# Half weight loads, a short sum on GpSimd and a conditional block without ScalarE, in a kernel of attention and routed experts

## The chip, the core and the metric

The kernel runs on one core of a Trainium2 chip. Its engines work side by side, each on its own queue of instructions: TensorE (PE; its weight loads are shown apart as PEld), VectorE (DVE), ScalarE (ACT), GpSimd (POOL) and SyncE (SP). SP and POOL also issue DMA transfers, which run on the core's 16 DMA engines. The metric is the time of one execution on the device, in microseconds; lower is better. Before the change it is 411.5 us, the median of three runs (409.78, 411.5, 412.72).

## The reference

First comes attention over 8 batches of 8 heads, 576 positions and 64 columns a head, causal by blocks of 64 positions:

```python
scores = scale * np.matmul(q, k.transpose(0, 1, 3, 2))
scores = np.where(block_i >= block_j, scores, -1000000000.0)
attn = np.exp(scores - max);  attn = attn / (sum + 1e-09)
attn_out = np.matmul(attn, v)
```

Its output, as 8 x 576 rows of 512 columns, goes through one expert a row. Each of the 8 experts has a w1 of 512 x 1024 and a w2 of 1024 x 512. Which expert takes a row is found in order within a batch: a local gate decides whether the row takes its own best expert or that of the row before it.

```python
logits = x @ w_gate;  local_gate = sigmoid(x @ w_local)
e = argmax(logits[s]) if s == 0 or local_gate[s] < 0.5 else prev_e
out[s] = softmax(logits[s])[e] * (np.maximum(x[s] @ w1[e], 0.0) @ w2[e])
```

## The kernel before

**Attention: slots.** Two heads of one batch make a pair; there are 32 pairs, four a batch. The loop at L1198 has one slot for each pair. Slot i computes the scores of pair i (L972 to L977), takes their exponentials on ScalarE (L987), forms the products with v of pair i - 1 (`values`, L998 and L1007), and transposes q and k of pair i + 1 (L692, L925, L946). SyncE loads q and k of pair i + 2 (L867, L872) and v (L889, L892). GpSimd arranges q and k of pair i + 2 (`arrange`, L880). The exponentials of the first block of keys are in a tile S, those of the other blocks in a tile Pc. S rotates through three buffers and Pc through two.

**Sums of rows.** The denominators of the softmax are found by a matrix product over S (`half_batch`, L705), in every odd slot, for the pairs i - 3 and i - 2. So that S holds the whole sum, VectorE adds the other blocks onto it in `add_chunks`: three sums of the wide blocks (L1019), and one short sum of 64 x 128 elements for the last block (L1021), whose exponentials lie in the lower half of S's first 64 columns. `mask` then clears that corner of S with a memset (L1026). Slot i masks pair i - 1. GpSimd does it for 30 of the pairs: in even slots up to 16 ahead of `arrange`, in the others behind it. VectorE does it for pair 29 (in slot 30) and for pair 31 (after the loop).

**Routing.** The choice of experts is a long chain of small steps (`tokens`, `slots_first`, `slots_second`), written as a generator. The loop gives its steps to VectorE and TensorE by a fixed budget of weights at fixed points of each slot (L1145, `vector`, `routing`). Finished rows are transposed by TensorE (`rows_of_batch`), scaled by VectorE (L818) and stored to a buffer `x_rows` in HBM (L677). These stores are held back and issued by GpSimd at the end of a slot (`release`, L1262). The scores, the transposes for rows and the small products of the routing share three PSUM buffers, "sc".

**Weights.** w1 and w2 of all experts are kept in SBUF as bf16. `load_weights` (L105) loads one w1 (L107) or w2 (L111) of one expert by one DMA of GpSimd's queue, which casts from f32: 1024 KB as written. Experts 0 to 6 are loaded in the loop, one load in every second slot from 2 to 28, in the order w1 of expert 0, w2 of expert 0, w1 of expert 1 and so on (L1258). What the routing needs as scratch lies in the place of expert 7, and staged q and k lie in those of experts 6 and 7 of w2. So expert 7 comes last: its w1 out of the list `pending`, between the first gathers, as soon as the routing has the row indices of the first phase (L540, issued at L1255 of slot 29), its w2 at the end of slot 30 (L1270). The order on GpSimd's queue at the end of a slot is:

```python
            while pending:
                pending.pop(0)()

            if wload < 2 * E - 2 and i == 2 + 2 * wload:
                load_weights(*divmod(wload, 2))
```

and behind it `release`.

**Experts: tiles.** Rows are gathered by expert into tiles of 128 rows, by indirect DMAs of GpSimd (L651), and transposed by DMAs of SyncE (L1269, L1393). A tile takes 32 products with w1 (`first_mm`, L1093), a ReLU on ScalarE (L1096), eight products with w2 (`second_mm`, L1335), a scaling on ScalarE (L1340) and an indirect store by GpSimd (L1343). VectorE copies the w1 of the tile's expert, chosen by a register, to a fixed place ahead of it (L1078, L1297). As the expert is in a register, the first products with w2 wait for all loads of w2. TensorE does the first products of tiles 0 and 1 about the end of the loop and those with w2 behind them.

**The conditional block.** The number of tiles depends on the data. The last five possible tiles are in a conditional block (`more_tiles`, L1417), run if the count of tiles in use is high enough. It stands in the loop over tiles four tiles ahead of the last one of the list. All engines load the count (L1473) and branch on it (L1474). `xtrans` (L1081), which copies transposed rows out of PSUM, is called in this block alone; `first_mm` and `second_mm` are called in the block and in the loop.

Of the kernel before, what the change touches and what calls it, by code (L numbers as in the profile page):

```python
# [62 lines left out]
def kernel(  # L63
# [11 lines left out]
    nc = tc.nc  # L75
# [4 lines left out]
    ALU = mybir.AluOpType  # L80
# [21 lines left out]
    w1_bf = w_p.tile([P, E * KO1 * F], BF16, tag="w1", name="w1_bf")  # L102
    w2_bf = w_p.tile([P, E * FO * Dm], BF16, tag="w2", name="w2_bf")
    WE = KO1 * F
    def load_weights(e, layer):  # L105
        if layer == 0:
            nc.gpsimd.dma_start(  # L107
                out=w1_bf[:, e * WE:(e + 1) * WE].rearrange("p (do f) -> p do f", f=F),
                in_=moe_w1[e].rearrange("(do di) f -> di do f", di=P))
        else:  # L110
            nc.gpsimd.dma_start(  # L111
                out=w2_bf[:, e * WE:(e + 1) * WE].rearrange("p (fo d) -> p fo d", d=Dm),
                in_=moe_w2[e].rearrange("(fo fi) d -> fi fo d", fi=P))

    HP = H // 2
    NPAIR = B * HP
# [715 lines left out]
    with tc.tile_pool(name="atn_const", bufs=1) as cst, \  # L832
# [181 lines left out]
        def add_chunks(i):  # L1014
            if not 0 <= i < NPAIR:
                return
            for c in range(1, NC - 1):
                n = S - P * c
                nc.vector.tensor_add(Ss[i][:, :, P * c:], Ss[i][:, :, P * c:],  # L1019
                                     Pc[i % 2][:, :, POS[c]:POS[c] + n])  # L1020
            nc.vector.tensor_add(Ss[i][ST:, :, LAST:], Ss[i][ST:, :, LAST:], Ss[i][ST:, :, :ST])  # L1021

        def mask(i, engine):

            if 0 <= i < NPAIR:
                engine.memset(Ss[i][ST:, :, :ST], 0.0)  # L1026

        def sums_of(i):
# [52 lines left out]
        def xtrans(x, ps, xT):  # L1081
            for ko in range(KO1):
                nc.tensor.transpose(ps[:, ko, :], x[:, ko * P:(ko + 1) * P], id_b)
            nc.scalar.copy(xT, ps)
            return xT

        def first_mm(xT, w, hT, bank2, between=lambda: None):
            for half in range(2):
                ps = bank2()
                for fo in range(FO // 2):  # L1090
                    f0 = (half * (FO // 2) + fo) * P
                    for ko in range(KO1):
                        nc.tensor.matmul(ps[:, fo, :], lhsT=w[:, ko * F + f0:ko * F + f0 + P],  # L1093
                                         rhs=xT[:, ko, :],
                                         start=(ko == 0), stop=(ko == KO1 - 1))
                relu[0] = nc.scalar.activation(  # L1096
                    hT[:, half * (FO // 2):(half + 1) * (FO // 2), :], ps, func=AF.Relu)
                between()
            return hT

# [97 lines left out]
        for i in range(NPAIR):  # L1198
# [56 lines left out]
            while pending:  # L1255
                pending.pop(0)()

            if wload < 2 * E - 2 and i == 2 + 2 * wload:  # L1258
                load_weights(*divmod(wload, 2))
                wload += 1  # L1260
            if i < NPAIR - 1:
                release(queue=nc.gpsimd)  # L1262
# [28 lines left out]
    with ExitStack() as ffn:  # L1291
# [40 lines left out]
        def second_mm(ph, j, hT, ev, factor, y=None, between=lambda: None):  # L1332
            ps = f_ps.tile([P, Dm], F32, tag="ps_y", name="ps_y")
            for fo in range(FO):
                nc.tensor.matmul(ps, lhsT=hT[:, fo, :],  # L1335
                                 rhs=w2_bf[:, bass.ds(ev + fo * Dm, Dm)],
                                 start=(fo == 0), stop=(fo == FO - 1))
# [76 lines left out]
        def part(o, n, k):  # L1414
            return old[:, o:o + n].rearrange("p (k n) -> p k n", k=k)

        def more_tiles():  # L1417

            o = WE + Dm + FO * P
            x, y = (old[:, o:o + 2 * n].bitcast(F32) for n in (XW, Dm))  # L1420
            factor = old[:, o + 2 * Dm:o + 2 * Dm + 2].bitcast(F32)
            for ph, j in more:
                e = expert(ph, j)

                nc.vector.memset(x, 0.0)
                gather(ph, j, x)
                w = weights_at(old[:, :WE], e)
                nc.vector.tensor_copy(factor, factor_of(x))
                xT = xtrans(row_of_x(x), ps_x(), part(WE, Dm, KO1))
                hT = first_mm(xT, w, part(WE + Dm, FO * P, FO), ps_h)  # L1430
                second_mm(ph, j, hT, e, factor, y)


        holding[0] = True
        for i, (ph, j) in enumerate(tiles):
# [34 lines left out]
            if i == behind_tile:  # L1470

                nc.gpsimd.drain()
                n = nc.values_load(used[0:1, 0:1], min_val=0, max_val=E * BS)  # L1473
                with tc.If(n > NS[1] - MORE, label="more"):  # L1474
                    more_tiles()
        i = len(tiles) - 1
# [37 lines left out]
```

## Time and profile before

| | us |
|---|---|
| median of three runs | 411.5 |
| profiled execution | 408.54 |
| its span in the profile | 406.5 |
| busy: TensorE | 392.6 (97%) |
| busy: VectorE | 242.2 (60%) |
| busy: ScalarE | 228.7 (56%) |
| busy: GpSimd | 196.1 (48%) |

Times within the profile are counted from the start of the span. The attention loop takes about the first 257 us, the experts the rest. The granted clock of TensorE is at full speed in all slices. In a row of a timeline stand the start, the length, the engine, the line, the operation, the tile written and those read; at its end, in brackets, stand how long the engine had been idle before it and what ended that. "q" behind an engine's name is its sequencer, which issues instructions, waits and branches. q0 is the DMA queue of GpSimd, q1 that of SyncE; its row gives packets, MB and the share that the packets took of the 16 engines' time.

### The profile page before, as it was taken

Reading aid. Unit: us, or ns where it says so; the run is one execution under the profiler, and the core shown is the slowest. Engines: PE = TensorE matmul, PEld = TensorE weight load, DVE = VectorE, ACT = ScalarE, POOL = GpSimd, SP = SyncE. Lnnn points to the kernel's source line nnn. Section 1 sums busy time; section 2 is a strip of 40 time slices with the busy share of each in tenths; the row PEclk is TensorE's granted clock in tenths of the full one; section 3 lists DMA queues with packets and bytes.
Section 4 is the critical chain, followed back from the end, with each engine's and each line's share of the span. In section 5 each row is a group of like instructions: output and inputs, shape, how many; then the busy total and the mean of one; then the engine's idle time right before and its main releaser. Section 6 shows DMA issues by size and latency. Waiting matters only on the chain. (4 is left out here: it accounts for less than half of the span.)

```text
span 406.5 us, 14547 instructions
## 1 busy us (share of the span) xinstructions
PE 392.6 (97%) x5834; PEld 285.5 (70%) x5834; DVE 242.2 (60%) x505; ACT 228.7 (56%) x391; POOL 196.1 (48%) x250
## 2 busy tenths in 40 slices
PE   9999999999999999999998998998999999999985
PEld 7667677677677677667766666666777777777763
DVE  2463564564564577967899975977887333333320
ACT  3758557567557557657647465333545555555542
POOL 1244251342341342582632363074776888888833
PEclk9999999999999999999999999999999999999999
DMA  6588989999999979999989689944763645655532
GB/s 178 142 190 194 216 172 222 201 201 228 194 202 210 183 183 246 174 202 244 170 192 237 136 155 192 151 109 120 166 168 97 170 135 148 154 149 149 128 99 78
DMA packets 108819, 69.97 MB, mean 172 GB/s; under 512 B 74847, under 2 KB 100255, under 8 KB 108752
## 3 DMA queue, kind: packets, MB, share of 16 engines
q0 software_dynamic: 19200, 34.84, 41.6%
q1 hardware_dynamic: 89552, 34.19, 37.2%
q8 instruction: 48, 0.79, 0.8%
q14 instruction: 19, 0.16, 0.1%
HBM read 66.88 MB, written 14.70 MB: 201 GB/s over the span
## 5 line engine op out<-in xcount | busy, mean ns | idle before, releaser
L1019 DVE TENSOR_TENSOR S<-S,Pc 128x896 f32<-128x896 f32 (+2 forms) x96 | 84.0, 875 | 23.9 <-PE o L998 19.1
L977 PE MATMUL sc<-qkT 64*64 64x224 f32 (+6 forms) x1536 | 91.6, 367 | 0.0
L1297 DVE COPY w1c<-w_bf 128x4096 bf16 x36 | 44.3, 1231 | 55.6 <-PE ps_h L1093 52.8
L1093 PEld LDWEIGHTS <-w1c 128*128 128x128 bf16 x1152 | 67.2, 98 | 9.1 <-issue 1.3
L880 POOL COPY w_bf<-w_bf 128x512 f32<-128x512 f32 x61 | 43.9, 737 | 60.8 <-DMA w_bf<-in_k_dram 33.0
L977 PEld LDWEIGHTS sc<-qkT 64*64 64x64 f32 x1536 | 70.5, 134 | 3.7 <-issue 2.5
L1335 PE MATMUL ps_y<-w_bf,hT 128*128 x296 | 69.9, 379 | 1.0 <-DMA w_bf<-in_moe_w_dram 1.0
L987 ACT ACTIVATE Pc<-sc 128x448 f32<-128x448 f32 (+1 forms) x96 | 68.1, 716 | 0.0
L1093 PE MATMUL ps_h<-xT,w1c 128*128 128x128 bf16 x1088 | 66.3, 219 | 1.3 <-ACTq L1474 1.1
L1343 POOL DMA_INDIRECT out_dram<-y,idx x37 | 56.2, 1519 | 22.0 <-ACT y L1340 12.2
L651 POOL DMA_INDIRECT xg<-x_rows,idx x38 | 47.1, 1239 | 31.3 <-issue 13.9
L1096 ACT ACTIVATE hT<-ps_h 128x512 bf16<-128x512 f32 x76 | 45.3, 597 | 26.2 <-PE ps_h L1093 24.6
L998 PE MATMUL o<-Pc,v 128*64 128x320 f32 (+2 forms) x512 | 57.3, 366 | 0.0
L998 PEld LDWEIGHTS o<-Pc,v 128*64 128x64 f32 x512 | 34.6, 137 | 24.1
L1340 ACT ACTIVATE y<-ps_y,xg 128x512 f32<-128x512 f32 x37 | 25.4, 687 | 45.5 <-PE ps_y L1335 39.1
L987 ACT ACTIVATE S<-sc 128x576 f32<-128x576 f32 x64 | 42.0, 656 | 12.6 <-PE sc L977 12.1
L1335 PEld LDWEIGHTS <-hT 128*128 128x128 bf16 x296 | 27.5, 98 | 27.3 <-issue 1.0
L1011 ACT COPY oT<-o 128x576 f32<-128x576 f32 x32 | 20.5, 641 | 35.7 <-PE o L1007 35.7
L1026 POOL MEMSET S<- 64x128 f32 x30 | 6.0, 200 | 69.8 <-DVE S L1021 40.7
L818 DVE TENSOR_TENSOR xg<-trx,rs 128x512 bf16<-128x512 f32 (+1 forms) x31 | 20.2, 685 | 25.9 <-PE trx L692 25.8
L998 PE MATMUL o<-S,v 128*64 128x192 f32 (+1 forms) x256 | 34.7, 392 | 0.3 <-ACT qkT L925 0.3
L714 ACT COPY LT<-trg 128x320 f32<-128x320 f32 x15 | 6.4, 426 | 44.4 <-PE trg L705 44.4
(313 smaller groups left out, 467.4 us busy)
## 6 DMA issues: line engine op xcount, KB each, us to landing
w_bf<-in_moe_w_dram POOLq DMA_DIRECT2D x16, 1024.0 KB, 9.9
w_bf<-in_k_dram SPq DMA_DIRECT2D x32, 256.0 KB, 3.4
w_bf<-in_q_dram SPq DMA_DIRECT2D x32, 256.0 KB, 7.7
v<-in_v_dram SPq DMA_DIRECT2D x64, 128.0 KB, 5.8
x_rows<-xg POOLq DMA_DIRECT2D x24, 128.0 KB, 8.1
qkl<-in_k_dram SPq DMA_DIRECT2D x32, 32.0 KB, 3.8
qkl<-in_q_dram SPq DMA_DIRECT2D x32, 32.0 KB, 5.7
vl<-in_v_dram SPq DMA_DIRECT2D x32, 32.0 KB, 7.4
```

The source lines that it names most:

```text
L651: st = nc.gpsimd.indirect_dma_start(out=x, out_offset=None, in_=x_dram[:rows], in_offset=bass.IndirectOffsetOnAxis(ap=row_of(ph, j), axis= ...
L880: copies[j](m, raws[i][1 + j].rearrange("p h j d -> p j h d"))
L977: nc.tensor.matmul(to[:, col + skip:col + n], lhsT=t[r, 0, k0:k0 + ST], rhs=t[r, 1, q0 + skip:q0 + n], start=True, stop=True)
L987: nc.scalar.activation(exps_at(i, c, q0, n, rows), ps[rows, :, col:col + n], func=AF.Exp, scale=scale_attn)
L998: nc.tensor.matmul(po[64 * h:64 * h + 64, VO + q0:VO + q0 + n], lhsT=vs[i][c][:, h, :], rhs=exps_at(i, c, q0, n, slice(0, P))[:, h, :], st ...
L1019: nc.vector.tensor_add(Ss[i][:, :, P * c:], Ss[i][:, :, P * c:], Pc[i % 2][:, :, POS[c]:POS[c] + n])
L1093: nc.tensor.matmul(ps[:, fo, :], lhsT=w[:, ko * F + f0:ko * F + f0 + P], rhs=xT[:, ko, :], start=(ko == 0), stop=(ko == KO1 - 1))
L1096: relu[0] = nc.scalar.activation(hT[:, half * (FO // 2):(half + 1) * (FO // 2), :], ps, func=AF.Relu)
L1297: ended["w"] = nc.vector.tensor_copy(w, w1_bf[:, bass.ds(ev[i], WE)])
L1335: nc.tensor.matmul(ps, lhsT=hT[:, fo, :], rhs=w2_bf[:, bass.ds(ev + fo * Dm, Dm)], start=(fo == 0), stop=(fo == FO - 1))
L1340: nc.scalar.activation(y, ps, func=AF.Copy, scale=factor)
L1343: st = nc.gpsimd.indirect_dma_start(out=out_flat, out_offset=bass.IndirectOffsetOnAxis(ap=row_of(ph, j), axis=0), in_=y, in_offset=None, b ...
```

## The change

Three things are changed.

1. `load_weights` can load a half of a w1 or w2: the halves divide the rows of the matrix by the groups of 128 of them, so the runs in memory stay as long as they were. The 14 loads of the loop become 28 halves, one in each slot from 2 to 29. Expert 7 is loaded whole, as before.
2. The short sum (L1021) moves from `add_chunks` to `mask`, ahead of its memset and on the same engine: GpSimd for 30 pairs, VectorE for pairs 29 and 31.
3. In the conditional block the work of ScalarE (the copy in `xtrans`, the ReLU, the scaling) goes to VectorE, and ScalarE neither loads the count nor branches.

```diff
-    def load_weights(e, layer):
-        if layer == 0:
-            nc.gpsimd.dma_start(
-                out=w1_bf[:, e * WE:(e + 1) * WE].rearrange("p (do f) -> p do f", f=F),
-                in_=moe_w1[e].rearrange("(do di) f -> di do f", di=P))
-        else:
...
+    def load_weights(e, layer, half=None):
+        w, x, n = ((w1_bf, moe_w1, F), (w2_bf, moe_w2, Dm))[layer]
+        r = slice(0, WE // n) if half is None else slice(half * WE // n // 2, (half + 1) * WE // n // 2)
+        nc.gpsimd.dma_start(
+            out=w[:, e * WE:(e + 1) * WE].rearrange("p (o n) -> p o n", n=n)[:, r],
+            in_=x[e].rearrange("(o i) n -> i o n", i=P)[:, r])
...
-            nc.vector.tensor_add(Ss[i][ST:, :, LAST:], Ss[i][ST:, :, LAST:], Ss[i][ST:, :, :ST])
 
         def mask(i, engine):
 
             if 0 <= i < NPAIR:
+                engine.tensor_tensor(Ss[i][ST:, :, LAST:], Ss[i][ST:, :, LAST:],
+                                     Ss[i][ST:, :, :ST], op=ALU.add)
                 engine.memset(Ss[i][ST:, :, :ST], 0.0)
...
         def xtrans(x, ps, xT):
...
-            nc.scalar.copy(xT, ps)
+            nc.vector.tensor_copy(xT, ps)
...
-        def first_mm(xT, w, hT, bank2, between=lambda: None):
+        def first_mm(xT, w, hT, bank2, between=lambda: None, scalar=True):
...
+                if scalar:
+                    relu[0] = nc.scalar.activation(to, ps, func=AF.Relu)
+                else:
+                    nc.vector.tensor_single_scalar(to, ps, 0.0, op=ALU.max)
...
-            if wload < 2 * E - 2 and i == 2 + 2 * wload:
-                load_weights(*divmod(wload, 2))
+            if wload < 4 * E - 4 and i == 2 + wload:
+                load_weights(*divmod(wload // 2, 2), wload % 2)
                 wload += 1
...
-            nc.scalar.activation(y, ps, func=AF.Copy, scale=factor)
+            if scalar:
+                nc.scalar.activation(y, ps, func=AF.Copy, scale=factor)
+            else:
+                nc.vector.tensor_scalar(y, ps, factor, None, op0=ALU.mult)
...
+        MORE_ON = tuple(getattr(mybir.EngineType, e) for e in ("PE", "DVE", "Pool", "SP"))
...
-                hT = first_mm(xT, w, part(WE + Dm, FO * P, FO), ps_h)
-                second_mm(ph, j, hT, e, factor, y)
+                hT = first_mm(xT, w, part(WE + Dm, FO * P, FO), ps_h, scalar=False)
+                second_mm(ph, j, hT, e, factor, y, scalar=False)
...
-                n = nc.values_load(used[0:1, 0:1], min_val=0, max_val=E * BS)
+                n = nc.values_load(used[0:1, 0:1], min_val=0, max_val=E * BS, engines=MORE_ON)
                 with tc.If(n > NS[1] - MORE, label="more"):
                     more_tiles()
```

More of the change, by code (lines that the diff above doesn't have):

```diff
@@ L104 @@
     WE = KO1 * F
-    def load_weights(e, layer):
-        if layer == 0:
-            nc.gpsimd.dma_start(
-                out=w1_bf[:, e * WE:(e + 1) * WE].rearrange("p (do f) -> p do f", f=F),
-                in_=moe_w1[e].rearrange("(do di) f -> di do f", di=P))
-        else:
-            nc.gpsimd.dma_start(
-                out=w2_bf[:, e * WE:(e + 1) * WE].rearrange("p (fo d) -> p fo d", d=Dm),
-                in_=moe_w2[e].rearrange("(fo fi) d -> fi fo d", fi=P))
+    def load_weights(e, layer, half=None):
[4 more added lines that the diff above has]
+            in_=x[e].rearrange("(o i) n -> i o n", i=P)[:, r])
     HP = H // 2
@@ L1095, in first_mm @@
                                          start=(ko == 0), stop=(ko == KO1 - 1))
-                relu[0] = nc.scalar.activation(
-                    hT[:, half * (FO // 2):(half + 1) * (FO // 2), :], ps, func=AF.Relu)
+                to = hT[:, half * (FO // 2):(half + 1) * (FO // 2), :]
+                if scalar:
+                    relu[0] = nc.scalar.activation(to, ps, func=AF.Relu)
+                else:
+                    nc.vector.tensor_single_scalar(to, ps, 0.0, op=ALU.max)
                 between()
@@ L1330, in last_mm, with second_mm @@
             tc.add_to_no_dep_group("stores", st.ins)
-        def second_mm(ph, j, hT, ev, factor, y=None, between=lambda: None):
+        def second_mm(ph, j, hT, ev, factor, y=None, between=lambda: None, scalar=True):
             ps = f_ps.tile([P, Dm], F32, tag="ps_y", name="ps_y")
```

## The prediction

> **What bounds the kernel now.** I read the page first, then the list of what TensorE waited for, then the timelines of TensorE, VectorE and GpSimd around each of those waits, and last the DMA queues there.
>
> ```profile
> span 406.5 us, 14547 instructions
> PE 392.6 (97%) x5834; PEld 285.5 (70%) x5834; DVE 242.2 (60%) x505; ACT 228.7 (56%) x391; POOL 196.1 (48%) x250
> ```
>
> TensorE is busy for 392.6 of 406.5 us. So an edit on VectorE, ScalarE or GpSimd is worth only what it takes from, or adds to, the short list of TensorE's own waits (line, whom it waited for, us, times, longest):
>
> ```profile
> PE sc L975 <- DVE xg L818: 1.8, 1, 1.8
> PE ps_h L1093 <- ACTq L1474: 1.1, 1, 1.1
> PE rtb L340 <- DVE S L337: 1.0, 1, 1.0
> PE ps_y L1335 <- DMA w_bf<-in_moe_w_dram: 1.0, 1, 1.0
> ...
> PE rti L496 <- DVE w_bf L525: 0.2, 1, 0.2
> ```
>
> Each part of the change points at one of these. In time they stand here, with what ran ahead of them:
>
> ```profile
> 211.89 1.26 PE L705 MATMUL trg<-S,sel 128*32 128x320 f32 x16
> ...
> 216.63 0.67 PE L692 MATMUL trx<-id_f,oT 64*128 64x64 f32 x16
> ...
> 224.13 0.22 PE L975 MATMUL sc<-ones_b,minus 64*64 64x64 bf16 x2 [1.77 <-DVE xg L818]
> ...
> 262.69 1.89 PE L1335 MATMUL ps_y<-w_bf,hT 128*128 x8 [0.97 <-DMA w_bf<-in_moe_w_dram]
> ```
>
> From the first product to slot 28 no wait over 0.3 us is TensorE's, and none at all is for the q, k or v loads. What the change does there is covered; the sum is made at slots 26 to 31 and at the branch.
>
> **Part 1: the short sum leaves VectorE.** Of the 32 short sums (L1021), 30 go to GpSimd; those of pairs 29 and 31, which VectorE masks, stay on it. They are worth something where VectorE is late, which is the queue that ends in L818 ahead of 224.13. The first row groups the four sums between 189 and 218.3 us (min/median/max ns); the others are VectorE's timeline:
>
> ```profile
> L1021 DVE TENSOR_TENSOR S<-S x4: 289/400/511, 193.9 to 217.9; 64x128 f32<-64x128 f32 x4
> ```
> ```profile
> 189.56 0.68 DVE L818 TENSOR_TENSOR xg<-trx,rs 64x512 bf16<-64x512 f32 x1 [1.69 <-PE trx L692]
> ...
> 218.27 1.29 DVE L818 TENSOR_TENSOR xg<-trx,rs 128x512 bf16<-128x512 f32 x2
> ```
>
> VectorE waits last at 189.56 and then runs without a gap past 224. The four sums are 4 x 0.40 = 1.6 us of that queue. Not all of it comes through: the L818 at 218.27 needs the transposes that TensorE ends at 216.63 + 0.67 = 217.30, so it can come forward by 0.97 at most, and I take 0.9. All behind it shifts alike, so TensorE's 1.77 falls to about 0.9. One more short sum, that of slot 28, lies between there and L525, so the 0.2 of L496 goes too. **Gain 1.1 us** from 229 on; bounds 0 (GpSimd takes it back, below) and 2.0 (the whole 1.77 and 0.2).
>
> On GpSimd the sum has no row. The nearest are the memset behind it and a copy with four times its elements (the copy as min/median/max ns):
>
> ```profile
> 210.65 0.20 POOL L1026 MEMSET S<- 64x128 f32 x1 [0.29 <-DVE S L1021]
> ```
> ```profile
> L880 POOL COPY w_bf<-w_bf x61: 608/622/1292, 6.9 to 235.5; 128x512 f32<-128x512 f32 x61
> ```
>
> So 0.2 to 1.3 us, and I take 0.3, near the memset of its shape: 30 x 0.3 = 9 us more on an engine that is 48% busy. The new wait is GpSimd's, for the last L1019 sum; the memset waited for L1021, behind that, so it begins no later. Queued behind it are the memset, then the arranging copies or the weight load, and TensorE's row sums, which read the masked tile. The tightest place that I find is this memset against the L705 row at 211.89: it ends at 210.85, 1.0 us before the row sums. A sum of 0.3 is covered; without that cover TensorE pays what it takes over 1.0. The Trainium skill (GPSIMD Engine Reference, Engine selection) says that a two-input elementwise operation is about twice as slow on GpSimd and belongs on VectorE. By it the sum would take an estimated 0.6 us, twice the 0.29 of VectorE, still inside the cover; no row here shows a two-input operation on GpSimd.
>
> **Part 2: weight loads in halves.** 14 loads in slots 2, 4, ..., 28 become 28 in slots 2 to 29, so half a load sits in every slot and the second half of each pair comes one slot later. Their issues are 14 more. A whole one takes GpSimd 0.8 to 0.93, a 128 KB store 1.16 / 2 = 0.58:
>
> ```profile
> 241.76 0.83 POOL L107 DMA_DIRECT2D w_bf<-in_moe_w_dram  x1
> 242.90 1.04 POOL L651 DMA_INDIRECT xg<-x_rows,idx  x1 [0.30 <-issue]
> 244.25 1.01 POOL L651 DMA_INDIRECT xg<-x_rows,idx  x1 [0.31 <-issue]
> 246.66 1.16 POOL L677 DMA_DIRECT2D x_rows<-x  x2 [1.40 <-DVE x L818]
> ...
> 248.38 0.93 POOL L111 DMA_DIRECT2D w_bf<-in_moe_w_dram  x1
> ```
>
> Extra issue time is 14 x 0.6 to 0.9, about 8 to 13 us, in slots where GpSimd waits for others. It matters where the last half falls. That is the second half of w2 of expert 6, now in slot 29. In the code slot 29 first issues the pending gathers and the load of expert 7's w1 (the first three rows) and then this half, so it comes at about 245.3, into the idle 1.40 ahead of 246.66: the issue is covered. Its data is not. It stands in GpSimd's DMA queue ahead of the x stores and of expert 7's w2 (248.38), for which TensorE waits at 262.69. The queue in two stretches: 40 to 54 us, where it carries one whole w2 load and nothing else, and 244 to 262; then all engines from 250 to 262 and from 262 to 266 (last two columns: DMA share, GB/s):
>
> ```profile
> q0 software_dynamic: 1040, 1.05, 50.2%
> ```
> ```profile
> q0 software_dynamic: 1776, 2.66, 93.8%
> ```
> ```profile
> 250.00:262.00 12.00, 11.27 (x181) 8.77 (x181) 10.31 (x20) 6.19 (x13) 0.20 (x1) 1.00 1.29 182
> 262.00:266.00 4.00, 3.31 (x29) 1.47 (x30) 2.65 (x9) 1.21 (x3) 1.55 (x2) 1.00 0.23 63
> ```
>
> A whole load costs 50.2% of 14 us = 7.0 us of all engines, a half 3.5. From 244 to 262 this queue is busy 93.8% of the time and the share falls only when the w2 load has landed, so nothing absorbs the half: the landing moves by **+3.5 us**, and TensorE's wait ends with it. Bounds: 0 if the engines fit it in after all, 7.0 if a half costs what a whole one does. The Trainium skill (DMA: Bandwidth & Descriptors, Anatomy of one DMA) gives a DMA from GpSimd about 2.0 us plus bytes over 436 GB/s. By it a half would be an estimated 3.2 us (0.52 MB) and the sum 0.3 less; but a whole one would be 4.4, where the row has 7.0, so the row decides.
>
> The gain of part 1 also brings forward the indices, hence the gathers and this whole queue, so at 262.69 the two net to 3.5 - 1.1 = +2.4. The x stores of 246.66 stand behind the half as well, and slot 31's rows reuse their buffers, so part of this may show as an earlier wait, of VectorE at L818 and of TensorE at L1093; the w2 load is last either way. The later TensorE waits (L340) hang on products behind this point and move with it.
>
> In slots 2 to 28 the same bytes flow with shorter bursts; TensorE waits for none of them, so zero. If that cover were gone, a half would be 3.5 a slot.
>
> **Part 3: no ScalarE in the conditional block.** The block's body does not run: behind the branch TensorE goes on with the loop's own tile. In TensorE's timeline, its weight loads', and the branch line (min/median/max ns, first and last start):
>
> ```profile
> 384.66 1.95 PE L1093 MATMUL ps_h<-xT,w1c 128*128 128x128 bf16 x32
> ...
> 389.41 1.95 PE L1093 MATMUL ps_h<-xT,w1c 128*128 128x128 bf16 x32 [1.08 <-ACTq L1474]
> ```
> ```profile
> 384.44 1.99 PEld L1093 LDWEIGHTS <-w1c 128*128 128x128 bf16 x32
> ...
> 388.75 0.10 PEld L1093 LDWEIGHTS <-w1c 128*128 128x128 bf16 x1 [0.91 <-DVE w1c L1297]
> ```
> ```profile
> L1474 DVEq EVENT_SEMAPHORE  x2: 21/21/21, 384.4 to 384.5; - x2
> ...
> L1474 ACTq EVENT_SEMAPHORE  x1: 17/17/17, 389.3 to 389.3; - x1
> ```
>
> The first product starts when ScalarE's branch posts at 389.3. TensorE itself is through its own branch and loads the first weight at 388.75; one tile earlier product followed load by 384.66 - 384.44 = 0.22. So it starts at 388.97. VectorE, which takes ScalarE's part, posted at 384.5, so what is late next is TensorE's own branch. **Gain 0.4 us**; bounds 0 (the branch still binds ScalarE) and 1.1.
>
> **The sum.** +3.5 - 1.1 - 0.4 = **+2.0 us**. The profiled execution took 408.54 us, 2.96 under the median of the three timed runs (411.5). I add the 2.0 to the median: **413.5 us**, 0.5% more.
>
> **The rivals.**
> *The half is hidden.* A share of 1.29 counts overlapping packets, so the engines may have room that it doesn't show, or the stores and transposes yield. Then only the gains stay: 411.5 - 1.5 = 410.0. Against it: the queue's 93.8%.
> *A half costs as much as a whole load (the other side, slower by more than 1%).* At slot 29, if fixed cost rather than bytes fills the queue, the landing moves by 7.0: +7.0 - 1.5 = +5.5, 417.0. It passes 1% from a delay of 5.6 on. Against it: 1040 packets of one size make up the 7.0 us, and a half has 520 of them. The same page's rule of batching to 1 MiB or more speaks for this rival; the trace shows no half.
> *GpSimd takes the gain back.* The new sum reads two tiles while VectorE works. L1021 takes 289 or 511 ns, and L880 608 to 1292, so the two engines do slow each other. Were all of the 1.1 lost, +3.5 - 0.4 = +3.1: 414.6.
> *Faster by over 1%.* If all four waits that the parts touch vanished, 1.77 + 0.2 + 0.97 + 1.08 = 4.0: 407.5, just 1%. Nothing reaches further.
>
> **How the numbers follow.** The timed runs spread over 0.7%, so about 1% (4.1 us) is what can be told from no change. Forecast 0.57 (its own range 412 to 415), hidden 0.20, whole cost 0.13, gain lost 0.07, faster by 1% 0.03. Within 1%: 0.57 + 0.20 + 0.07 = 0.84; slower 0.13; faster 0.03. The range 409.6 to 416.5 takes in the first, most of the second and the fourth, with the runs' own spread, and leaves out most of the 417 case.
>
> **What would show it.** Part 1: the wait of L975 near 0.9 and a GpSimd sum near 0.3 ahead of each memset. Part 2: a half issued near 244 to 245, and waits for it of about 4.5 us instead of 0.97 (0.97 + 3.5, the lead cancelling out), at L1335 and in part at L1093. Part 3: no wait for ScalarE at L1474 and the first product 0.2 us behind its weight load. I am wrong if L1335 and L1093 there wait under 2 us together, if L975 still waits 1.8, or if new waits of TensorE show in slots 2 to 28.

## The result and the profile after

The changed kernel takes 413.77 us, the median of 22 runs (410.47 to 415.70), against 411.81 us, the median of 22 runs of the kernel before beside it. The ratio is 1.006, with a 95% interval of 1.004 to 1.008: slower by about 2.5 us (0.006 x 411.81). The ratios here leave disturbed executions out, which the medians still hold.

The profiled execution took 412.05 us. Its page begins (busy time, share of the span, instructions):

```profile
span 410.2 us, 14593 instructions
...
PE 393.1 (96%) x5834; PEld 284.2 (69%) x5834; DVE 233.8 (57%) x475; ACT 226.6 (55%) x391; POOL 216.4 (53%) x294
```

TensorE does the same work, so the 3.7 us that the span has grown are waits and a stretch of 3.4 us at about half the clock (below). VectorE is 8.4 us less busy and GpSimd 20.3 us more. TensorE's waits in this kernel (line, whom it waited for, us, times, longest; `second_mm` is now L1336, `first_mm` L1091, the chunk-mask product L972, the row sums L702):

```profile
PE ps_y L1336 <- issue: 2.2, 1, 2.2
PE ps_h L1091 <- PEq L1103: 1.7, 1, 1.7
PE rtb L337 <- DVE S L334: 1.4, 1, 1.4
...
PE sc L972 <- DVE xg L815: 0.8, 1, 0.8
...
PE ps_h L1091 <- DVE x L815: 0.8, 1, 0.8
```

"issue" at L1336 is a semaphore of the w2 loads in TensorE's queue. In time the rows stand here (start, us, the wait in brackets):

```profile
179.54 1.70 PE L702 MATMUL trg<-S,sel 128*32 128x320 f32 x16
...
222.18 0.22 PE L972 MATMUL sc<-ones_b,minus 64*64 64x64 bf16 x2 [0.84 <-DVE xg L815]
...
233.72 0.40 PE L493 MATMUL rti<-w_bf 128*128 128x70 bf16 x7 [0.51 <-ACT Pc L984]
...
256.71 1.07 PE L1091 MATMUL ps_h<-S,Pc 128*128 128x128 bf16 x16 [0.75 <-DVE x L815]
...
262.62 2.71 PE L1336 MATMUL ps_y<-w_bf,hT 128*128 x8 [2.16 <-issue]
265.26 2.09 PE L702 MATMUL trg<-S,sel 128*32 128x320 f32 x16
...
392.72 1.95 PE L1091 MATMUL ps_h<-xT,w1c 128*128 128x128 bf16 x32 [1.72 <-PEq L1103]
```

Set against the same rows of before, each start less the start there, this gives a ledger:

| row of after | start less that of before | what happened since the last one |
|---|---|---|
| 179.54 (row sums, slot 23) | -1.5 | the first 12 us went faster, which the change does not touch (last section) |
| the row behind them | -1.0 | the row sums took 1.70, not 1.26: they stood for their memset |
| 222.18 (chunk mask) | -1.95 | part 1's gain, 0.93 |
| 226.96 (first rti row) | -2.23 | L496's wait is gone, 0.28 |
| 256.71 (half of tile 0) | -1.26 | a new wait for the x rows |
| 262.62 (w2) | -0.07 | the longer wait for w2 |
| first product behind 265.26 | +1.6 | 2.71 and 2.09 us for work that took 1.89 and 1.28: the clock |
| 387.32 (ahead of the branch) | +2.7 | later waits, a few tenths each |
| 392.72 (behind it) | +3.3 | TensorE's branch, 0.65 longer |

### The profile page after: what moved, and what is told of

It reads as the page before. It is cut to its first block, busy times and chain, and to the rows that moved or that the text cites. A ratio compares the mean times of both kernels' runs of the same rounds, so it can differ in the third digit from the quotient of the medians.

```text
span 410.2 us, 14593 instructions
## 1 busy us (share of the span) xinstructions
PE 393.1 (96%) x5834; PEld 284.2 (69%) x5834; DVE 233.8 (57%) x475; ACT 226.6 (55%) x391; POOL 216.4 (53%) x294
## 4 chain that ended last, share of the span: by engine, by line
PE 75%; issue 7%; DMA 6%; DVE 5%; POOL 4%; SPq 1%; ACT 1%; POOLq 1%; DVEq 0%; ACTq 0%
PE o L995 19%; PE sc L974 18%; PE ps_h L1091 10%; PE ps_y L1336 10%; PE trg L702 6%; PE kq L689 4%; DMA x_rows<-x 3%; DMA out_dram<-y,idx 2%; PE trx L689 2%; PE o L1004 2%; POOL xg L648 2%; POOL out_dram L1347 2%; PE o L689 2%; PE sc L969 1%; DMA w_bf<-in_q_dram 1%
## 5 line engine op out<-in xcount | busy, mean ns | idle before, releaser
L1016 DVE TENSOR_TENSOR S<-S,Pc 128x896 f32<-128x896 f32 (+2 forms) x96 | 86.2, 898 | 26.2 <-PE o L995 18.2
L877 POOL COPY w_bf<-w_bf 128x512 f32<-128x512 f32 x61 | 48.3, 808 | 54.4 <-DMA w_bf<-in_k_dram 33.4
L1091 PEld LDWEIGHTS <-w1c 128*128 128x128 bf16 x1152 | 67.2, 98 | 10.8 <-issue 4.1
L1336 PE MATMUL ps_y<-w_bf,hT 128*128 x296 | 70.7, 382 | 2.2 <-issue 2.2
L648 POOL DMA_INDIRECT xg<-x_rows,idx x38 | 49.2, 1293 | 43.5 <-issue 16.1
L1091 PE MATMUL ps_h<-xT,w1c 128*128 128x128 bf16 x1088 | 66.5, 219 | 2.3 <-PEq L1103 1.7
L1347 POOL DMA_INDIRECT out_dram<-y,idx x37 | 44.9, 1215 | 23.5 <-issue 9.5
L1336 PEld LDWEIGHTS <-hT 128*128 128x128 bf16 x296 | 27.6, 98 | 28.8 <-issue 2.8
L1022 POOL TENSOR_TENSOR S<-S 64x128 f32<-64x128 f32 x30 | 14.5, 484 | 47.8 <-DVE S L1016 28.6
L943 ACT COPY qkT<-kq 128x1024 f32<-128x1024 f32 x30 | 30.9, 1029 | 0.4 <-PE trx L689 0.4
```

The costliest lines, as they stand in the source:

```text
L648: st = nc.gpsimd.indirect_dma_start(out=x, out_offset=None, in_=x_dram[:rows], in_offset=bass.IndirectOffsetOnAxis(ap=row_of(ph, j), axis= ...
L877: copies[j](m, raws[i][1 + j].rearrange("p h j d -> p j h d"))
L1336: nc.tensor.matmul(ps, lhsT=hT[:, fo, :], rhs=w2_bf[:, bass.ds(ev + fo * Dm, Dm)], start=(fo == 0), stop=(fo == FO - 1))
L1347: st = nc.gpsimd.indirect_dma_start(out=out_flat, out_offset=bass.IndirectOffsetOnAxis(ap=row_of(ph, j), axis=0), in_=y, in_offset=None, b ...
```

## The experiments

The kernels of each of the three groups below ran on one chip beside the kernel before. The medians of before differ by chip (408.97, 409.99 and 414.18 us), so only the ratios are compared. "Distance to w2" below is worked out from two rows of each profile: the start of tile 0's second products less that of the x7 rti row, 262.69 - 235.95 = 26.74 in the kernel before. Intervals stand in square brackets behind the ratios.

### Each part alone, and the half taken out of slot 29

**e1_halves**: before, with part 2 alone.

```diff
-            if wload < 2 * E - 2 and i == 2 + 2 * wload:
-                load_weights(*divmod(wload, 2))
+            if wload < 4 * E - 4 and i == 2 + wload:
+                load_weights(*divmod(wload // 2, 2), wload % 2)
```

> The kernel before with part 2 alone: weight loads in halves, one a slot. Forecast's theory (the last half stands ahead of expert 7's w2 in GpSimd's DMA queue, one stall at the first products with w2): +3.5 us by the bytes, at least +2, and TensorE's granted clock dips for a few us behind the longer wait; the wait ahead of slot 29 at L975 stays 1.8 us. Rival (the halves are free, what the whole change lost was lost elsewhere, for instance at the branch): within 0.5 us of before. Rival (a half costs as much as a whole load): +5 us or more.

Measured: 412.71 us, ratio 1.0112 [1.0081, 1.0144]. That is +4.6 us (0.0112 x 408.97), between +3.3 and +5.9: the +3.5 of the theory lies inside, free halves are excluded, and the price of a whole load is not. The waits for the x rows and w2 were 1.29 and 2.68 us; the distance to w2 was 29.38. The dip of the granted clock that the theory had behind them did not come.

**e2_sum**: before, with part 1 alone.

```diff
-            nc.vector.tensor_add(Ss[i][ST:, :, LAST:], Ss[i][ST:, :, LAST:], Ss[i][ST:, :, :ST])
...
+                engine.tensor_tensor(Ss[i][ST:, :, LAST:], Ss[i][ST:, :, LAST:],
+                                     Ss[i][ST:, :, :ST], op=ALU.add)
                 engine.memset(Ss[i][ST:, :, :ST], 0.0)
```

> The kernel before with part 1 alone: the short sum goes to GpSimd for 30 pairs. Forecast's theory (VectorE's queue before slot 28 gets shorter): -1.1 us, the wait of L975 falls from 1.8 to about 0.9 us and that of the rti products vanishes. Rival (GpSimd's sum slows VectorE by as much): within 0.3 us of before.

Measured: 412.9 us from six runs, ratio 1.0129 [1.0085, 1.0173]: slower, which no theory had. The wait at 224.13 did fall to 0.85. But in slot 24 the memset came late, and with it the row sums of slot 25. GpSimd's timeline of e2_sum, then TensorE's:

```profile
195.65 1.17 POOL L880 COPY w_bf<-w_bf 128x512 f32<-128x512 f32 x2 [6.85 <-DMA w_bf<-in_k_dram]
196.90 0.45 POOL L1025 TENSOR_TENSOR S<-S 64x128 f32<-64x128 f32 x1
197.41 0.20 POOL L1027 MEMSET S<- 64x128 f32 x1
```
```profile
196.78 0.71 PE L705 MATMUL trg<-S,sel 128*32 128x320 f32 x4
197.66 1.27 PE L705 MATMUL trg<-S,sel 128*32 128x320 f32 x12 [0.18 <-POOL S L1027]
```

GpSimd waited 6.85 us for a k load before its copies. In before this memset was done 2.0 us ahead of the row sums; here they lost 0.9 us, between their fourth and fifth product.

**e3_branch**: before, with part 3 alone.

```diff
-                n = nc.values_load(used[0:1, 0:1], min_val=0, max_val=E * BS)
+                n = nc.values_load(used[0:1, 0:1], min_val=0, max_val=E * BS, engines=MORE_ON)
```

and the three operations of the block on VectorE.

> The kernel before with part 3 alone: ScalarE neither loads the count nor branches. Forecast's theory (ScalarE's post ended the wait): -0.4 us, and the distance of the first products of the tiles around the branch falls from 4.75 to 4.3 us. Rival from the profile of the whole change (that distance was 5.40 there): +0.6 us, TensorE's own branch becomes longer when ScalarE stays out.

Measured: 408.8 us, ratio 1.0005 [0.9968, 1.0042]. The time can't tell -0.4 from +0.6 us. The two tiles about the branch start 4.53 us apart instead of 4.75: a gain, of about half of what the theory had.

**e4_early**: after, with w2 of expert 6 loaded whole in slot 28, so that slot 29 carries no half.

```diff
-                load_weights(*divmod(wload // 2, 2), wload % 2)
-                wload += 1
+                last = wload == 4 * E - 6
+                load_weights(*divmod(wload // 2, 2), None if last else wload % 2)
+                wload += 1 + last
```

> The whole change, but w2 of expert 6 is loaded whole in slot 28 as before, so nothing of it is left for slot 29; the other 26 halves stay. Forecast's theory (only the half that stands in slot 29 costs): -1.5 us against before, or -1.1 or less if the branch gains nothing; expert 7's w2 lands about 2 to 3.5 us sooner than with the whole change, no dip of the granted clock there. Rival (halves cost in other slots as well, or the half was hidden): as the whole change, +2 us.

Measured: 408.27 us, ratio 0.9996 [0.9963, 1.003]. With the half out of slot 29 the loss is gone: the rival's +2 us (1.005) lies outside the interval, and the -1.1 to -1.5 of the theory just inside. TensorE does not wait for w2 at all (distance 25.90):

```profile
235.07 0.40 PE L493 MATMUL rti<-w_bf 128*128 128x70 bf16 x7 [0.51 <-ACT Pc L984]
...
260.97 1.89 PE L1337 MATMUL ps_y<-w_bf,hT 128*128 x7
```

But a wait showed that no theory had, in slots 21 to 23. GpSimd's timeline of e4_early, then TensorE's:

```profile
169.29 0.79 POOL L108 DMA_DIRECT2D w_bf<-in_moe_w_dram  x1
170.08 4.72 POOL L674 DMA_DIRECT2D x_rows<-factors  x7
178.72 0.55 POOL L674 DMA_DIRECT2D x_rows<-factors  x1 [3.93 <-PE rta L327]
179.32 1.17 POOL L877 COPY w_bf<-w_bf 128x512 f32<-128x512 f32 x2
180.57 0.45 POOL L1022 TENSOR_TENSOR S<-S 64x128 f32<-64x128 f32 x1
181.08 0.20 POOL L1024 MEMSET S<- 64x128 f32 x1
```
```profile
181.33 1.27 PE L702 MATMUL trg<-S,sel 128*32 128x320 f32 x12 [1.67 <-POOL S L1024]
```

At the end of slot 21 GpSimd issues eight small stores: the softmax factors of four batches, four stores of 2.0 KB and four of 0.2 KB. In before they went through in 5.28 us, and this slot had no load. GpSimd's timeline of before, then TensorE's:

```profile
171.35 5.28 POOL L677 DMA_DIRECT2D x_rows<-factors  x8 [0.52 <-DVE rs L794]
...
178.21 0.20 POOL L1026 MEMSET S<- 64x128 f32 x1
```
```profile
181.01 1.26 PE L705 MATMUL trg<-S,sel 128*32 128x320 f32 x16
```

In e4_early a half of expert 4's w2 stands ahead of them, and the eighth store is held for 3.93 us. The copies, the sum and the memset of slot 22 queue behind it, and TensorE's row sums of slot 23 wait for the memset. After has the same, milder; GpSimd's timeline of after (the later rows are the half of slot 29 and what follows it):

```profile
170.09 4.73 POOL L674 DMA_DIRECT2D x_rows<-factors  x7
177.36 0.55 POOL L674 DMA_DIRECT2D x_rows<-factors  x1 [2.54 <-PE o L995]
177.95 1.17 POOL L877 COPY w_bf<-w_bf 128x512 f32<-128x512 f32 x2
179.21 0.45 POOL L1022 TENSOR_TENSOR S<-S 64x128 f32<-64x128 f32 x1
179.72 0.20 POOL L1024 MEMSET S<- 64x128 f32 x1
...
243.04 0.82 POOL L108 DMA_DIRECT2D w_bf<-in_moe_w_dram  x1
244.71 1.15 POOL L674 DMA_DIRECT2D x_rows<-x  x2 [0.85 <-DVE x L815]
...
246.43 0.93 POOL L108 DMA_DIRECT2D w_bf<-in_moe_w_dram  x1
```

The memset ends at 179.92 there, after the row sums' first products (179.54), which is why they took 1.70 us. The releaser that the profile names for the eighth store differs from profile to profile (a product here, the landing of a weight load in e1, e5, e7, e9, e10 and e12). The landing fits in all: where the profile gives that of slot 21's half, 8.8 us after its issue in e1 and 9.2 in e4, it comes at 178.05 and 178.49, and the eighth store is issued 0.26 and 0.23 us later; in all eight profiles with halves it is issued 1.0 to 1.4 us after the half's last packet ended. That the store needs an entry of GpSimd's DMA queue which this landing frees is inferred.

### The sum again, a double dose, filler products, two pairs

**e6_sum_again**: the kernel of e2_sum once more.

> The kernel before with part 1 alone (the short sum on GpSimd), the same kernel that measured 1.013 [1.0085, 1.0173] from six runs. Theory (the sum takes cover away from the memset: GpSimd ends its copies late whenever a k load lands late, and TensorE's row sums at 181, 197, 212 and 229 us then wait for the memset; in the earlier profile the row sums at 197 gained 0.9 and the ones at 230 another): again slower than before, ratio 1.003 to 1.013, with waits of TensorE for the memset's line. Rival (the earlier six runs were the upper end of the scatter): ratio 0.997 to 1.002, as the gain of 0.9 at the line of 224.13 alone would give.

Measured: 411.53 us from 12 runs, ratio 1.0019 [0.9978, 1.0059]. So the 1.3% of e2 did not come back, and neither expectation is excluded. Two groups of runs of one kernel lie further apart than their intervals allow, so a ratio from six or seven runs (e1, e2, e5, e7) is less sure than its interval says. The profile shows both sides of the account: the row sums of slot 25 again stood for the memset and lost 1.0 us, those of slot 23 lost nothing, and the chunk mask and the rti row gained 0.93 and 0.28.

**e7_whole29**: after, with both halves of expert 6's w2 in slot 29 and none in slot 28.

```diff
-                load_weights(*divmod(wload // 2, 2), wload % 2)
+                if wload < 4 * E - 6:
+                    load_weights(*divmod(wload // 2, 2), wload % 2)
+                elif wload == 4 * E - 5:
+                    load_weights(*divmod(wload // 2, 2))
```

> The kernel after, but both halves of expert 6's w2 are loaded as one in slot 29, and slot 28 loads nothing: the half's dose doubled at the same place. Theory (what counts is the bytes ahead of the x stores and of expert 7's w2 in GpSimd's queue, 2 to 3.5 us a half): TensorE's waits at the first and second products of tile 0 grow from 0.75 + 2.16 by another 2 to 3.5 us, ratio 1.011 to 1.016 against the kernel before. Rival (a load costs its place in the queue, whatever its size): the same waits and the same time as the kernel after, ratio 1.006.

Measured: 414.77 us, ratio 1.0117 [1.0071, 1.0162]. TensorE's timeline:

```profile
235.95 0.40 PE L493 MATMUL rti<-w_bf 128*128 128x70 bf16 x7 [0.51 <-ACT Pc L984]
...
263.88 1.89 PE L1091 MATMUL ps_h<-S,Pc 128*128 128x128 bf16 x16 [6.24 <-DVE x L815]
...
269.54 0.81 PE L1339 MATMUL ps_y<-w_bf,hT 128*128 x2
```

And VectorE's:

```profile
262.54 1.29 DVE L815 TENSOR_TENSOR x<-trx,rs 128x512 bf16<-128x512 f32 x2 [6.89 <-DMA x_rows<-x]
```

The x stores wait behind the whole load, VectorE's next rows reuse their buffers and wait for them, so the wait shows at the first products, 6.24 us, and w2 is there when they end (distance 33.59). No half, a half and two halves in slot 29 give -0.2, +2.5 and +4.8 us (the ratios 0.9996, 1.006 and 1.0117, times the medians of before): about 2.5 us a half. That is what bytes in a queue do, and the rival of a fixed place (1.006) lies outside the interval.

**e5_fill**: after, with 36 small products ahead of tile 0's second products.

```diff
+            for _ in range(36 if (ph, j) == (0, 0) else 0):
+                nc.tensor.matmul(ps[:, :P], lhsT=id_b, rhs=id_b, start=True, stop=True)
```

> The kernel after, with 36 small products of 128x128 written into the tile that the waiting second product will overwrite, ahead of tile 0's second products. They run while TensorE would otherwise stand waiting for w2 at 262.6; nothing else is changed. Theory (the idle time is what halves the granted clock from 263.5 on): the clock stays 1.0 there, tile 0's eight second products take 1.89 us again instead of 2.71, the row sums behind them 1.28 instead of 2.09, and the time falls by about 1.6 us against the kernel after, ratio near 1.002 against the kernel before. Rival (the dip has nothing to do with the idle time): the dip is there as before, and the time is the kernel after's, ratio near 1.006, or up to 2 us more if the filler outlasts the wait.

Measured: 417.71 us, ratio 1.0223 [1.0167, 1.028]. There is no halved clock at 260 to 270, as the theory had it, and the second products took 1.89 us. But the waits moved to a place far behind. TensorE's waits in e5_fill:

```profile
PE ps_h L1091 <- PEq L1103: 3.5, 1, 3.5
PE ps_h L1091 <- DVE x L815: 2.6, 1, 2.6
PE ps_h L1091 <- issue: 2.3, 1, 2.3
```

The first and the third stand right behind the conditional branch, where the clock halved too: about 7 us there. TensorE's branch itself took 3.69 us, 0.40 in after. Both expectations missed the time, and the run says nothing on what the halved clock costs.

**e8_pairs**: before with part 3, and the short sum on GpSimd for pairs 24 and 26 alone.

```diff
+            if i not in (24, 26):
+                nc.vector.tensor_add(Ss[i][ST:, :, LAST:], Ss[i][ST:, :, LAST:], Ss[i][ST:, :, :ST])
...
+                if i in (24, 26):
+                    engine.tensor_tensor(Ss[i][ST:, :, LAST:], Ss[i][ST:, :, LAST:],
+                                         Ss[i][ST:, :, :ST], op=ALU.add)
```

> The kernel before with part 3, and with the short sum on GpSimd for pairs 24 and 26 alone: their two sums lie in VectorE's queue ahead of 224.13 (0.4 us each), and behind their memsets no row sum of TensorE follows at once. Loads as in the kernel before. Theory (part 1's gain is real where VectorE is late, and its cost comes from the pairs whose row sums follow the memset): the wait of the chunk-mask product at 224.13 falls from 1.77 to about 1.0 us, no new wait for the memset; ratio 0.998. Rival (GpSimd's sum costs wherever it stands): a new wait for the memset's line or none gained, ratio 1.002 or more.

Measured: 409.1 us, ratio 0.9984 [0.9948, 1.002]. The chunk mask waits 0.8 and nothing waits for the memset: two sums of 30 give the whole gain of part 1 at that place. A wait that nobody expected is new in this profile, 1.64 us at 193.25 for a copy of ScalarE. A difference in time is not shown, since the interval holds 1, and the rival's 1.002 is at its edge.

### The change again, without its sum, an earlier load, fewer filler products

**e9_again**: the kernel after, unchanged.

> The kernel after once more, unchanged, for a second profile. Theory (TensorE's 1.72 us for its own branch and the halved clock behind w2 are what this kernel does): the branch wait is again near 1.7 (two tiles' first products 5.4 apart), tile 0's second products again wait some 2 us and take 2.7 us; ratio 1.006. Rival (both belong to the one profiled execution): the branch wait is 0.8, as in the three other kernels with part 3 (products 4.47 apart), and the second products take 1.89; ratio again 1.004 to 1.008, as the wait for the half alone gives it.

Measured: 415.12 us, ratio 1.0037 [0.9993, 1.008], which holds 1.006 and also 1. Its waits, and TensorE's row sums of slot 23:

```profile
PE ps_h L1091 <- DVE x L815: 2.2, 1, 2.2
PE ps_h L1091 <- PEq L1103: 1.8, 1, 1.8
PE trg L702 <- POOL S L1024: 1.4, 1, 1.4
```
```profile
181.76 1.27 PE L702 MATMUL trg<-S,sel 128*32 128x320 f32 x12 [1.38 <-POOL S L1024]
```

The branch wait came back, and so did the halved clock, one window earlier (260.4 to 263.8). There it fell on first products ahead of the wait for w2, which hid part of it: the second products waited 0.29 and took 1.89, where the theory had 2 and 2.7. The memset of slot 22 came later than in the first profile of this kernel.

**e10_nosum**: after without part 1.

```diff
-                engine.tensor_tensor(Ss[i][ST:, :, LAST:], Ss[i][ST:, :, LAST:],
-                                     Ss[i][ST:, :, :ST], op=ALU.add)
```

and the short sum back in `add_chunks`.

> The kernel after without part 1: the short sum back on VectorE for every pair; halves and branch as in the kernel after. Theory (part 1 gives 0.9 at the line of 224.13 and 0.2 behind it, the half then sets the end again, so that a later index takes most of the gain's place): the chunk-mask product waits 1.7 again, the first and second products of tile 0 wait 3 to 4 us together, ratio 1.008. Rival (part 1 costs more than it gives, by the memset that comes late): ratio 1.002 or less.

Measured: 415.51 us, ratio 1.0075 [1.0033, 1.0117]. The chunk mask waits 2.0 again. The first and second products of tile 0 waited 2.23 + 0.18 = 2.4 us, not the 3 to 4 of the theory. The rival's 1.002 is outside the interval, so part 1 does not cost more than it gives by that much. Whether it gives anything is not shown: the intervals of 1.0037 and 1.0075 overlap.

**e11_last27**: e8_pairs with w2 of expert 6 in slot 27.

```diff
-            if wload < 2 * E - 2 and i == 2 + 2 * wload:
+            if wload < 2 * E - 2 and i == 2 + 2 * wload - (wload == 2 * E - 3):
```

> A version meant to be faster than both: whole loads as in the kernel before, but the last of the 14 (w2 of expert 6) in slot 27 in place of 28, the short sum on GpSimd for pairs 24 and 26 alone, and part 3. Theory (what the queue carries late in the stage sets the landing of expert 7's w2): the wait for w2 of tile 0, 0.6 to 1.5 us in the five profiles with whole loads in slot 28, goes below 0.3; ratio 0.994 to 0.997. Rival (slot 27 has no room: GpSimd's issues or the k loads are late there, and TensorE's row sums wait for the memset): a new wait of 0.5 us or more between 210 and 232 us, ratio 0.999 or more.

Measured: 413.83 us, ratio 0.9989 [0.9945, 1.0032]. No wait for w2 is left in its profile, but e2 and e4 had none either, with a whole load in slot 28 (the expectation counts e2 among those that waited). New waits for v loads are there, 2.76 us the longest, at 232.38. That execution took 420.26 us, 6.4 over the median, so no size is read from it. Neither expectation is excluded. A version that beats the kernel before was not found.

**e12_fill9**: after, with nine filler products of 512 columns.

```diff
+            for _ in range(9 if (ph, j) == (0, 0) else 0):
+                nc.tensor.matmul(ps, lhsT=id_b, rhs=hT[:, :Dm // P, :], start=True, stop=True)
```

> The kernel after with 9 filler products of 128x512 in place of the 36 small ones: the same 2 us of TensorE ahead of tile 0's second products, with a quarter of the instructions. Theory (the idle time halves the clock, and the 36 added instructions moved what TensorE has to fetch behind the branch): no halved clock between 258 and 270 us unless the first products wait long, the branch wait is back at 0.8 to 1.7, and the ratio is 1.003 to 1.006. Rival (filler products themselves cost 7 us at the branch): a branch wait of over 3 us again, ratio near 1.02.

Measured: 415.31 us, ratio 1.0052 [1.0014, 1.0091]; the branch wait was 0.9. Time, branch wait and clock are as the theory had them, and the rival's 1.02 falls. In windows of time (length, busy time of PE, PEld, DVE, ACT, POOL, granted clock, DMA share, GB/s), first after, then e12_fill9:

```profile
260.10:263.50 3.40, 1.24 (x12) 0.68 (x10) 2.80 (x8) 1.08 (x2) 0.00 (x0) 1.00 0.72 145
263.50:267.00 3.50, 3.50 (x21) 0.97 (x19) 0.73 (x4) 0.69 (x1) 2.32 (x3) 0.51 0.13 38
```
```profile
260.10:263.50 3.40, 3.33 (x45) 2.44 (x39) 2.89 (x6) 1.52 (x4) 0.00 (x0) 1.00 1.32 169
263.50:267.00 3.50, 3.50 (x29) 1.39 (x27) 2.63 (x8) 1.06 (x2) 1.07 (x1) 1.00 0.20 62
```

Where TensorE has been busy, the clock stays at 1.00; where it stood 2.16 us of 3.4, it is 0.51 in the next 3.4. The filler saves no time that can be measured (1.0052 against 1.0037).

## Why the prediction was right, and where it was wrong

The time forecast, 413.5 us, +2.0, stands against 413.77 us and +2.5. Two terms of the sum were too large, the half and part 3, and losses that it lacked made up for them: slot 23, the clock and TensorE's branch.

**Part 1, the wait at the chunk mask: right.** Forecast about 0.9, measured 0.84, as the wait for transposes caps it; L496's 0.2 went. Together 0.93 + 0.28 = 1.2 us, forecast 1.1.

**Part 1, GpSimd's side: mis-sized, and its cover with it.** The sum took 0.45 us, not 0.3. The line of it in after (min/median/max ns):

```profile
L1022 POOL TENSOR_TENSOR S<-S x30: 447/450/1433, 22.3 to 251.4; 64x128 f32<-64x128 f32 x30
```

30 x 0.45 = 13.5 us, not 9; VectorE does the same shape in 0.29, a ratio of 1.55. The Trainium skill (GPSIMD Engine Reference, Engine selection), with about twice as slow, gives the estimate of 0.6, as far above 0.45 as my 0.3 was below. The step that failed is "the tightest place that I find is this memset against the L705 row at 211.89". I had checked the cover in a single profile. It is only as good as the arrival of k: in e2 and e6 the copies of slot 24 came late, and the row sums behind them lost 0.9 and 1.0 us where the cover had been 2.0. That the sum makes k late isn't shown: in e8, where VectorE still made the sum of that slot, GpSimd waited 7.60 us for the same load.

**Part 2, slots 2 to 28: wrong.** "TensorE waits for none of them, so zero" failed in slot 23, and new waits in slots 2 to 28 were one of my own signs of being wrong. I had asked what the bytes of a half delay and not what its place in GpSimd's queue delays. All eight profiles with halves show the eighth store held, for 2.1 to 3.9 us; the five others (e2, e3, e6, e8 and e11) lose nothing at the row sums of slot 23. What these rows lose (the time from their first product to their sixteenth, less that of before) is 1.1 and 0.8 us in the two kernels with halves and no sum (e1, e10), and 0.4 to 2.4 in the six with both (after, e4, e5, e7, e9, e12; mean 1.6). That part 1's 0.45 adds to it fits the means, but the ranges overlap. In the mean this loss takes about the whole gain of part 1. "GpSimd takes the gain back" was a rival, by contention; it came about by the queue. Contention doesn't show: VectorE's 96 wide sums (L1019) take 83.9 us in all in before and 83.9 in e2.

**Part 2, the half in slot 29: right in kind, too large by a third.** It was issued at 243.04 in after, ahead of the stores, and TensorE's waits for x rows and w2 were 0.75 + 2.16 = 2.9 us there, 4.0 in e1, forecast 4.5. The distance to w2 is 25.90 to 28.79 in the six profiles with no half in slot 29 (before, e2, e3, e4, e6, e8; mean 27.2), 28.90 to 29.92 in the six with one (after, e1, e5, e9, e10, e12; mean 29.5) and 33.59 with two. In e7 this start isn't the landing: the last packet of GpSimd's queue ahead of its pause began 1.8 us before it, and 0.7 to 0.9 before it in the thirteen other profiles. So a half moves the landing by 2.3, and the whole load by 33.59 - 27.2 - 1.0 = 5.4, where I had 3.5 and 7.0; timed, it is 2.5 a half. "Nothing absorbs the half" was too strong: without it the landing itself scatters over 2.9 us, and a part of the half may have fallen into that slack; why each byte cost less than I read from the queue's share stays open.

**Part 3: a gain of 0.25 where it showed, not 0.4.** The starts of the two tiles about the branch are 4.75 us apart in all four profiles with ScalarE's branch (before, e1, e2, e6), and 4.46 to 4.53 without it in e3, e4, e7 and e8. No wait for ScalarE is left, and what is late next is on TensorE's own queue. The step that failed is "one tile earlier product followed load by 0.22. So it starts at 388.97". Behind the branch TensorE first loads the number of the tile's expert into a register, and this row of before, which I had missed, shows it; TensorE's weight load in e3 stands under it:

```profile
L1102 PEldq TENSOR_LOAD <-et x1: 307/307/307, 388.8 to 388.8; - x1
```
```profile
388.58 0.10 PEld L1090 LDWEIGHTS <-w1c 128*128 128x128 bf16 x1 [0.98 <-DVE w1c L1297]
```

So the product follows the first weight load by 0.37 there (388.95 in e3), and by as much in e4, e7, e8 and after. With 0.37 the sum would have given 0.3 instead of 0.4, near the 0.22 to 0.29 measured.

In after, e9 and e10 the wait (PEq) is 1.7 to 1.9 instead of 0.8, and the distance 5.40 to 5.56. TensorE's branch line in after (min/median/max ns, first and last start):

```profile
L1480 PEldq EVENT_SEMAPHORE  x2: 51/51/51, 392.0 to 392.1; - x2
...
L1480 PEldq COMPARE_BRANCH  x1: 402/402/402, 389.9 to 389.9; - x1
```

From the branch's end at 390.3 to its next instruction at 392.0 nothing ran on TensorE's queue. In e3, e4, e7 and e8 that stretch was 0.8 to 1.0 us, with the same branch, and 1.1 in before. The chip alone doesn't set it: e9, e10 and e12 ran on one chip, and e12's wait was 0.9. So my bound of no loss fell in these executions; what ScalarE's part is worth where TensorE's queue is that late stays open.

**The clock was not in the sum.** The dip after the wait cost 0.82 + 0.81 = 1.6 us in after. It shows in after, e7, e9 and e10, and not in e1, e5 and e12, so it is a risk of a long wait and no fixed price.

As a sum for the profiled execution of after, from the ledger: -1.8 (start) + 0.3 (to slot 23) + 0.4 - 1.2 + 2.2 (x rows and w2) + 1.6 (clock) + 1.1 (later waits) + 0.65 (branch) = +3.3, the shift of its last tiles. Timed, the change gives +2.5, near my +2.0 because the half cost less, part 1 lost its gain in slot 23, part 3 gave little, and in some of the profiles the clock and the branch cost something too. That the place of the loss was right, the half ahead of expert 7's w2, is shown by e4 and e7; that the number was right is luck in good part, since these errors cancel.

## What to carry to other kernels

A load that is split takes no more bytes through its queue, but it stands in new places of it: go through every slot for what is issued behind it on that engine, stores and memsets too, and for who reads those. Put the last piece of a stream ahead of the transfers that set the end, and not behind the ones that start them; one slot earlier was worth the whole 0.6%. A cover read from one profile holds only as far as what feeds it arrives on time, so read it in several before an engine is given more work.

## What the runs showed of the hardware

**A wait of some 2 us can cost more than itself.** With TensorE busy 1.24 of 3.4 us, the granted clock was 0.51 to 0.50 for the next 3.4 us in after and e9; with 1.57 of 3.4 in e1 it stayed 1.00. In e8 it fell after 1.76 of 3.4, so busy time alone doesn't set the point. Where the wait falls matters too: counted from where the trace's clock record begins, all seven dips ahead of the kernels' last 3 us (after, e5, e7 to e11) begin at a whole number of steps of 3.413 us, and each lasts one or two of them. In e1 the wait was longer than in after, 2.68 us against 2.16, but it lay across the border of two such steps, with TensorE busy 1.57 and 2.49 us in them. The Trainium skill (TensorE: Matmul & The Clock Gate, What's actually happening) has the clock halved after an idle window of about 3.4 us; the 3.4 us of the dip agree, but the window ahead of it was not idle, only a third busy.

**The start varies.** The kernels do the same work in their first 12 us, yet after was 1.8 us ahead of before there. From 4 to 10 us 67 products run in the one and 106 in the other. A view of that window prints a granted clock of 1.00 for both, but the clock record in the trace begins at 10.2 us in before and at 4.1 in after, and so it goes with all: in eleven of the fourteen profiles the record begins at 4.1 to 6.0 us and the window holds 99 to 107 products, in three (before, e2, e7) it begins at 9.3 to 10.2 and the window holds 66 to 71. Single profiled spans differ by this much without any change.

**A branch that jumps costs TensorE more than its 0.4 us.** From its start to TensorE's next recorded instruction (L1474 and L1480 in the kernels before and after) pass 1.2 to 1.5 us in nine profiles, before among them, 2.1 to 2.2 in after, e9, e10 and e11, and 3.8 in e5. The branch itself takes 0.40 to 0.41 us in eleven of them, 0.9 in e6, 1.35 in e12 and 3.69 in e5. The 36 added products of e5 run 125 us ahead of the branch; with nine of them, in e12, it was 1.4. Since e12 ran on the chip of e9, this goes by execution and program. That instructions have to be brought from memory there is an inference and was not measured apart.
